# A linear-attention block with a token mixer: the product of Wo with the masked sums from high and low parts, and the steps around it in another order

## The chip, the cores and the metric

The kernel runs on one core of a Trainium2 chip. The metric is the device time of one execution in microseconds (us), the median over several runs. TensorE (PE in the profile; PEld are its weight loads) multiplies matrices, VectorE (DVE), ScalarE (ACT) and GpSimd (POOL) work on elements, and SyncE (SP) starts most of the DMA transfers. Each engine works through its own list of instructions in the order in which the program put them, and semaphores hold an instruction until what it reads is there.

## The reference, cut to what matters

A token array x of 2048 by 448 goes through a linear attention with 16 heads of width 28, and then through an MLP over the tokens. Six vectors of length 448 (shift, scale and gate of each half) come from a condition c.

```
h = layernorm(x) * (1 + ca) + sa
q, k, v = heads of h @ wqkv
phi(t) = where(t > 0, t + 1, exp(t)) + 1e-6
kv  = einsum("bhsd,bhse->bhde", phi(k), v)
z   = einsum("bhsd->bhd", phi(k))
num = einsum("bhqd,bhde->bhqe", phi(q), kv)
den = einsum("bhqd,bhd->bhq", phi(q), z)[..., None] + 1e-6
x = x + ga * ((num / den) @ wo)
h = layernorm(x) * (1 + cb) + sb
u = gelu(einsum("bsd,sf->bdf", layernorm(h), w1) + b1)
x = x + gb * transpose(einsum("bdf,fs->bds", u, w2) + b2)
```

## The kernel before, in words

The 2048 tokens are 16 tiles of 128 rows; an index behind a name is the tile (pkh14 is that of tile 14) or the group. There is no scheduler: each engine executes its instructions in the order in which the code issues them, so the place of a call in the code is its place in the queues of all engines that it uses. SBUF tiles come from two rings (`slot` and `tslot`), PSUM from eight banks (`bank`).

Most products are made from two parts of each operand: `split` (lines 82 to 84) lets ACT write a high part in the type fp32r and DVE write what is left, the low part. High times high, high times low and low times high are then three matmuls with fp32r operands. A matmul with plain fp32 operands needs no split; in the trace each such matmul of 448 columns is two records.

The parts that matter here, in the order of the program:

- The loop over t from 4 to 15 (line 682 on) projects the keys (`kp`), makes phi(k) (`ek`, `rk`, `pk`), its high and low parts (`pkh`, `pkl`), normalizes x (`xn`) and splits it (`xh`, `xl`), and lets PE add phi(k) transposed times x into four banks, `cacc` (`a_outer`, line 554). At the start of a step some early queries are finished (`a_phi_q`: `eq` and `rq` on ACT, `pq` on DVE, lines 465 to 470). At the end of steps 13, 14 and 15 DVE multiplies one group of 112 rows of Wo with the gate (line 779); the fourth group follows behind the loop (line 791).
- Behind the loop come the last four `a_outer`, the sum `pk` of all phi(k) and its parts `zh` and `zl`, and with them the matmuls `zp` (line 799). ACT scales the four banks (`cs`, line 808), DVE adds a correction, and PE multiplies with the V columns of wqkv into the bank `kvb` (line 818). DVE masks it: `kvm` (line 822), the sums within each head.
- Four fp32 matmuls multiply `kvm` with Wo (`wp`, line 968). ACT copies each result to SBUF (`wpg`, line 970), eight DMAs on SP's queue (line 977) rearrange the rows into `wpr`, and each of its four parts is split into `wph` and `wpl` (`wp_split`).
- The loop over i from 0 (line 988 on) takes one query tile per turn. PE transposes the scaled phi(q) (`tq`, line 863), multiplies it with the parts of `wpr` (`op`, lines 893 and 900), and still projects some queries (`qp`). For the tile i + 1 DVE makes `pd`, `den`, the reciprocal and the scaled phi(q) `pn` (lines 836 to 850); GpSimd adds a constant to `den` in between (line 843). The transpose of the tile then reads `pn` as its stationary operand. From turn 5 on PE also adds the first four blocks of the MLP (`up`, lines 950 to 952).
- The weights w1 of the MLP arrive as pieces `pr` of 128 by 512 (`load_to`) and are split into `ph` and `pl` (`split_to(n)` splits all pieces up to the n-th). Pieces 0 to 7 are split ahead of the query loop, in pairs: at line 794 (0, 1), after `zb` (2, 3), after two query projections (4, 5), and after `kvm` (6, 7).
- The scaled phi(q) of tile 0 is made behind `kvm` and behind pieces 6 and 7, just ahead of the four matmuls with Wo.

The MLP's other blocks and its second product fill the rest, from about 190 us to the end; the change does not touch them.

Of the kernel before, what the change touches and what calls it, by code (L numbers as in the profile page):

```python
# [9 lines left out]
F32R = mybir.dt.float32r  # L10
# [8 lines left out]
G = 112  # L19
# [32 lines left out]
def block_kernel(ctx: ExitStack, tc: tile.TileContext, x, xt, wqkv, wo, w1, b1, w2, c, wmod, wfirst, out):  # L52
# [19 lines left out]
    def tslot(name, dt=F32, parts=P, w=D):  # L72
        return tok.tile([parts, w], dt, name=name, tag="tok", padded_shape=[P, 512])


    def moving(new, name, dt=F32R, parts=P):
        return new(name, dt=dt, parts=parts, w=512)[:, 16:16 + D]

    def bank(name):
        return psum.tile([P, 512], F32, name=name, tag="bank")  # L80

    def split(full, hi, lo):
        nc.scalar.activation(hi, full, AF.Copy)  # L83
        nc.vector.tensor_sub(lo, full, hi.bitcast(F32))  # L84
# [219 lines left out]
    def load_to(i):  # L304
        while done["load"] < min(i, len(pieces)):
            k = done["load"]
            t, m, f0, n = pieces[k]
            raws[k] = slot(f"pr{k}", 512)
            nc.sync.dma_start(raws[k].rearrange("p (t f) -> p t f", t=m),
                              w1[t * P:(t + m) * P, f0 * P:(f0 + n) * P].rearrange("(t p) f -> p t f", p=P))  # L310
            done["load"] += 1
# [173 lines left out]
    def a_phi_q(keep=0):  # L485
        a_exp_q(keep)
        for t in sorted(eqs):
            pq[t] = phi_q(t)
# [28 lines left out]
    def a_pk_parts(t):  # L517
        if t not in pks:
            a_pk_high(t)
        a_pk_low(t)  # L520
# [156 lines left out]
    low()  # L677
    sum_end()
    a_split(7)
    wo_sb = []  # L680
    late = [t for t in range(NT) if t not in Q_EARLY.values()]
    for t in range(4, NT):
        if 5 < t < NT - 1:
            project(t + 1, 1, "kp")
        kp = close(t, 1) if t > 4 else kps[4]
        if t == 9:
            row_sum(0)
            row_bias(0)
        if t > 4:
            a_outer(t - KV_LAG)  # L690
        if t % 2 and 4 < t < NT - 2:
            a_transpose(t + 1)
        if t in Q_EARLY:
            a_q(Q_EARLY[t])
        if t == 12:
            mp = mod_sum2(2)
        pair = t % 2 and 7 < t + 3 < NT
        if pair:
            first, second, end = a_stats_dve((t + 3, t + 4))
            first(0)  # L700
        if 5 <= t < 9:
            w_low(0, t - 5)
        if pair:
            second(0)
        if 5 <= t < 9:
            row_part(0, t - 5)
        a_phi_q(t in Q_EARLY)
        if t == 9:
            a_exp(t, kp)
        if t % 2 and 4 < t < NT - 2:  # L710
            a_copy(t + 1)
            a_copy(t + 2)
        if t != 9:
            a_exp(t, kp)
        if 7 < t + 3 < NT:
            a_split_high(t + 3)
        a_pk_parts(t - 1)
        highs = HIGH_AT.get(t, (t - 2,))
        for i in highs[:1]:
            a_norm(i)  # L720
            a_high(i)
        if t % 2 == 0 and 4 < t < NT - 3:
            low = a_rows(t + 2)
        if t == 11:
            low2 = mod_high(2)
        for j, i in MOD_AT.get(t, ()):
            mod_add(j) if i is None else mod_part(j, i)
        if t == 14:
            low4()
        a_pk(t, kp)  # L730
        if t % 2 == 0 and 4 < t < NT - 3:
            low()
        if 7 < t + 3 < NT:
            a_split_low(t + 3)
        for i in highs[1:]:
            a_norm(i)
            a_high(i)
        if pair:
            first(1)
        for i in highs:  # L740
            a_low(i)
        if pair:
            second(1)
            end()
        sum_end()
        if 4 <= t < 8:
            w_high(0, t - 4)
            if t == 7:
                w_row(0)
        if t == 9:  # L750
            row_out(0)
        if t == 12:
            mod_out(2, mp)
            make_mask()
        if t in FETCH:
            load_xt(FETCH[t])
            load_x(FETCH[t])
        if 7 <= t < 11:
            mod_part(2, t - 7)
        if t == 10:  # L760
            mod_add(2)
        if t == 11:
            low2()
        if t == 13:
            low4 = mod_high(4)
        if t in (7, 10):
            load_mod(4 if t == 7 else 3)
        if t == 10:
            load_qkv(2, tslot)
        if t == 8:  # L770
            for g in range(4):
                w = tslot(f"wo{g}", parts=G)
                nc.sync.dma_start(w, wo[g * G:(g + 1) * G, :])
                wo_sb.append(w)
            b12 = cst.tile([P, NF + NT], F32, name="b12")
            nc.sync.dma_start(b12, b1)
            b1c, b2c = b12[:, :NF], b12[:, NF:]
        if t >= 13:
            nc.vector.tensor_mul(wo_sb[t - 13], wo_sb[t - 13], mods[2][:G])
        load_to(PRE_LOAD.get(t, 0))  # L780


    a_pk_parts(NT - 1)
    nc.vector.tensor_add(pksum[1], pksum[1], pksum[0])
    zs = (moving(slot, "zh"), moving(slot, "zl"))
    split(pksum[1], *zs)
    load_to(10)
    a_phi_q()
    a_outer(NT - 4)
    a_outer(NT - 3)  # L790
    nc.vector.tensor_mul(wo_sb[3], wo_sb[3], mods[2][:G])
    for i in (2, 3):
        mod_part(3, i)
    split_to(2)
    a_outer(NT - 2)
    a_outer(NT - 1)
    zp = bank("zp")
    for i, pk in enumerate(zs):
        nc.tensor.matmul(zp[:, :D], ones_r, pk, start=(i == 0), stop=(i == 1))
    zb = tslot("zb")  # L800
    nc.scalar.activation(zb, zp[:, :D], AF.Copy, bias=S * 1e-6)
    load_to(14)
    split_to(4)
    a_q(late.pop(0))
    csum = []
    for ch in range(4):
        csum.append(slot(f"cs{ch}"))
        nc.scalar.activation(csum[ch], cacc[ch][:, :D], AF.Identity, scale=col[1][:, ch:ch + 1])
        nc.vector.scalar_tensor_tensor(csum[ch], zb, col[0][:, ch:ch + 1], csum[ch], op0=ALU.mult, op1=ALU.add)
    a_phi_q()  # L810
    a_q(late.pop(0))
    split_to(6)
    mp = mod_sum2(4)
    kvb = bank("kvb")
    for ch in range(4):
        for g in range(4):
            s = slice(g * G, (g + 1) * G)
            nc.tensor.matmul(kvb[:G, s], raw_w[2, ch][:, s], csum[ch][:, s], start=(ch == 0 and g == 0),  # L818
                             stop=(ch == 3), skip_group_check=True)
    a_phi_q()  # L820
    kvm = slot("kvm", parts=G)
    nc.vector.tensor_mul(kvm, kvb[:G, :D], mask)
    mod_out(4, mp)
    load_to(PRE + MID + 3)
    split_to(8)
    Wpr, Wph, Wpl = [], [], []


    H2h, H2l = [None] * NT, [None] * NT
    pns, phs, ys, opb, sums, nms, nm2s, rss, vss = {}, {}, {}, {}, {}, {}, {}, {}, {}  # L830

    dens, prods, lasts = {}, {}, {}

    def b_prod(t):
# [13 lines left out]
    def b_scale(t):  # L848
        pn = pns.pop(t, None) or tslot(f"pn{t}", w=512)
        nc.vector.scalar_tensor_tensor(pn[:, :D].rearrange("p (h d) -> p h d", d=DH),  # L850
                                       pq[t].rearrange("p (h d) -> p h d", d=DH), 1e-6,
                                       dens.pop(t).unsqueeze(2).to_broadcast([P, H, DH]),
                                       op0=ALU.add, op1=ALU.mult)
        pns[t] = pn
        pq[t] = None

    def b_transpose(t):
        pn = pns.pop(t)
# [101 lines left out]
            del parts[k]  # L960

    a_q(late.pop(0))
    for fn in (b_prod, b_sum, b_eps, b_recip, b_scale):
        fn(0)
    mod_add(3)
    for g in range(4):
        wp = bank(f"wp{g}")
        nc.tensor.matmul(wp[:G, :D], kvm[:, g * G:(g + 1) * G], wo_sb[g], start=True, stop=True)  # L968
        wpg = tslot(f"wpg{g}", parts=G)
        nc.scalar.activation(wpg, wp[:G, :D], AF.Copy)  # L970
        if g == 0:
            Wpr += [tslot(f"wpr{ch}") for ch in range(4)]
        for ch in range(4):
            r0, r1 = max(ch * P, g * G), min(ch * P + P, (g + 1) * G)
            for p0 in (0, 64) if ch == 3 else (0,):
                if r0 < r1:
                    nc.sync.dma_start(Wpr[ch][p0 + r0 - ch * P:p0 + r1 - ch * P], wpg[r0 - g * G:r1 - g * G])
# [10 lines left out]
    for i in range(NT + LAG):  # L988
# [72 lines left out]
        if i == 0:  # L1061
            for ch in range(4):
                wp_split(ch)
        a_phi_q(nq if late else 0)
        load_to(max(14 + (i + 1) // 2, 12 + max(0, i - 6) + max(0, i - 14)))
        if res or norm1:
# [320 lines left out]
```

## Time and profile before

| what | value |
|---|---|
| time, median of 3 runs | 433.37 us (433.33 to 433.41) |
| the profiled execution's own time | 434.09 us |
| its span, first to last instruction | 432.4 us |
| share of the span with PE busy | 99% |
| share with DVE busy | 84% |
| share with ACT busy | 65% |

Times in rows of the trace count from the start of the span. A row of the timeline gives start, length, engine, line, operation, what it writes and reads, shapes and count, and in brackets how long the engine had been idle before and what it had waited for. Records of matmuls overlap: each lasts longer than the distance to the next, and the distance is what counts.

### The profile page before, as it was taken

How to read it: one execution, taken by the hardware profiler on the slowest of the kernel's cores; microseconds unless marked ns; L12 is line 12 of the kernel's file. 1: busy time of each engine (PE TensorE's matmuls, PEld its weight loads, DVE VectorE, ACT ScalarE, POOL GpSimd, SP SyncE). 2: the span in 40 equal slices, each digit the busy share in tenths (PEclk: the TensorE clock that was granted, in tenths of full speed). 3: DMA queues.
4: the chain of work that ended last, by engine and by line, in shares of the span. 5: the costliest groups of instructions: out<-in, count | busy, mean ns of one | idle time of the engine just before them, and what ended most of it. 6: DMA issues, size and time to landing. Idle time of an engine off the chain costs nothing.

```text
span 432.4 us, 7216 instructions
## 1 busy us (share of the span) xinstructions
PE 427.9 (99%) x2331; PEld 398.0 (92%) x2331; DVE 365.1 (84%) x814; ACT 278.9 (65%) x595; POOL 120.1 (28%) x199
## 2 busy tenths in 40 slices
PE   8999999999999999999999999999999999999997
PEld 8888899999899999999999999999999999999996
DVE  4899987889899999998579695739799998898894
ACT  5799869658578899996755263537464664655550
POOL 4345444300026577775200000010113131132010
PEclk9999999999999999999999999999999999999999
DMA  8997997565300036354427461577379977986431
GB/s 282 385 337 162 239 264 162 89 206 193 86 1 0 26 74 148 74 125 97 145 85 244 142 212 50 166 203 210 79 193 214 207 159 159 214 170 144 85 46 41
DMA packets 63797, 66.14 MB, mean 153 GB/s; under 512 B 4816, under 2 KB 55312, under 8 KB 63760
## 3 DMA queue, kind: packets, MB, share of 16 engines
q1 hardware_dynamic: 54688, 50.90, 37.8%
q0 software_dynamic: 8784, 14.32, 20.8%
q10 hardware_dynamic: 288, 0.46, 0.4%
q8 instruction: 18, 0.29, 0.3%
q14 instruction: 19, 0.16, 0.1%
HBM read 46.30 MB, written 7.34 MB: 124 GB/s over the span
## 4 chain that ended last, share of the span: by engine, by line
PE 97%; DVE 1%; ACT 1%; issue 0%
PE y L1183 19%; PE up L951 10%; PE up L950 10%; PE up L952 10%; PE y L1184 9%; PE cacc L554 7%; PE qp L432 7%; PE op L893 7%; PE kp L432 6%; PE op L900 1%; PE warm L188 1%; PE tq L863 1%; PE qp L439 1%; PE kvb L818 1%; PE wp L968 1%; PE rowb L287 1%
## 5 line engine op out<-in xcount | busy, mean ns | idle before, releaser
L950 PE MATMUL up<-h2h,ph 128*128 128x448 f32 x224 | 81.2, 362 | 0.0
L951 PE MATMUL up<-h2l,ph 128*128 128x448 f32 x224 | 81.2, 362 | 0.0
L952 PE MATMUL up<-h2h,pl 128*128 128x448 f32 x224 | 80.8, 361 | 0.0
L1138 POOL DMA_DIRECT2D a<-a x16 | 14.2, 964 | 142.6 <-DMA pr<-in_B_w_dram 76.7
L950 PEld LDWEIGHTS up<-h2h,ph 128*128 128x128 f32 x224 | 42.0, 188 | 3.1
L952 PEld LDWEIGHTS up<-h2h,pl 128*128 128x128 f32 x224 | 41.9, 187 | 3.0
L951 PEld LDWEIGHTS up<-h2l,ph 128*128 128x128 f32 x224 | 42.0, 188 | 2.3
L84 DVE TENSOR_TENSOR pl<-pr,ph 128x512 fp32r<-128x512 f32 x46 | 30.7, 688 | 2.6 <-ACT ph L83 1.7
L1189 ACT ACTIVATE cc<-y 128x448 f32<-128x448 f32 x24 | 13.0, 546 | 26.7 <-PE y L1184 26.7
L1102 DVE TENSOR_TENSOR u<-u,mod 128x448 f32<-128x448 f32 x14 | 8.7, 623 | 23.0 <-ACT u L1101 22.8
L83 ACT ACTIVATE ph<-pr 128x512 fp32r<-128x512 f32 x46 | 27.6, 623 | 0.8 <-PE up L952 0.5
L1101 ACT ACTIVATE u<-up,b 128x448 f32<-128x448 f32 x14 | 8.8, 625 | 25.4 <-PE up L952 24.9
L432 PE MATMUL kp<-wh,hh 128*128 128x448 f32 x64 | 23.8, 377 | 0.0
L554 PE MATMUL cacc<-pkh,xh 128*128 128x448 f32 x64 | 23.6, 369 | 0.0
L432 PE MATMUL qp<-wh,hh 128*128 128x448 f32 x64 | 23.5, 368 | 0.0
L1203 POOL DMA_DIRECT2D out_dram<-yt x14 | 12.7, 909 | 37.3 <-DVE yt L1194 27.9
L843 POOL TENSOR_SCALAR den<-den 128x16 f32<-128x16 f32 x16 | 8.8, 548 | 44.2 <-DVE den L840 44.2
L554 PE MATMUL cacc<-pkl,xh 128*128 128x448 f32 x56 | 20.3, 362 | 0.0
L893 PE MATMUL op<-wph,pth 128*128 128x448 f32 x48 | 18.7, 390 | 0.0
L1144 DVE TENSOR_TENSOR a<-a,s 128x512 f32<-128x512 f32 (+1 forms) x32 | 18.5, 622 | 0.0
L83 ACT ACTIVATE s2h<-s 128x512 fp32r<-128x512 f32 (+1 forms) x16 | 8.3, 569 | 15.5 <-DVE s L1144 15.5
L1183 PE MATMUL y<-ub,a11h 128*128 128x448 f32 x56 | 18.2, 375 | 0.0
(235 smaller groups left out, 1383.7 us busy)
## 6 DMA issues: line engine op xcount, KB each, us to landing
pr<-in_B_w_dram SPq DMA_DIRECT2D x56, 256.0 KB, 3.1
a<-in_B_w_dram SPq DMA_DIRECT2D x32, 256.0 KB, 4.8
a<-in_B_w_dram SPq DMA_DIRECT2D x32, 192.0 KB, 4.7
xt<-in_xt_dram SPq DMA_DIRECT2D x16, 256.0 KB, 5.0
x<-in_A_x_dram SPq DMA_DIRECT2D x16, 224.0 KB, 5.0
wm<-in_B_wmod_dram SPq DMA_DIRECT2D x16, 196.0 KB, 5.2
out_dram<-x SPq DMA_DIRECT2D x14, 224.0 KB, 2.3
out_dram<-yt POOLq DMA_DIRECT2D x14, 224.0 KB, 6.1
```

The lines of the kernel that those rows point to most:

```text
L83: nc.scalar.activation(hi, full, AF.Copy)
L84: nc.vector.tensor_sub(lo, full, hi.bitcast(F32))
L432: nc.tensor.matmul(pps[t, j][:, :D], a[:, ch * P:(ch + 1) * P], w, start=first, stop=False)
L554: nc.tensor.matmul(cacc[ch][:, :D], a[:, s], b, start=(t == 0 and i == 0), stop=(t == NT - 1 and i == len(todo) - 1))
L893: nc.tensor.matmul(opb[t][:, :D], a, b, start=(ch == n == 0), stop=False)
L950: nc.tensor.matmul(ps[:, :D], hi[:, sl], mh, start=first, stop=False)
L951: nc.tensor.matmul(ps[:, :D], hi[:, sl], ml, start=False, stop=False)
L952: nc.tensor.matmul(ps[:, :D], lo[:, sl], mh, start=False, stop=last)
L1138: nc.gpsimd.dma_start(w, a, accum_op=ALU.add)
L1144: nc.vector.tensor_tensor(w, raw2[q, a][i], raw2[q, b][i], op=op)
L1183: nc.tensor.matmul(ps[:, :D], h[:, s], w, start=opens and r == 0, stop=False, skip_group_check=True)
L1184: nc.tensor.matmul(ps[:, :HD], l[:, s], wh, start=False, stop=closes and r == PAIRS - 1, skip_group_check=True)
```

## The change

The four fp32 matmuls of Wo become twelve fp32r matmuls. For this the four groups of Wo are split (`wo_split`: `woh` on ACT, `wol` on DVE), groups 0 and 1 at the end of step 14 of the first loop, right behind the multiplication of group 1, groups 2 and 3 behind `zb`, where pieces 2 and 3 were split. `kvm` is split into `kvh` and `kvl`. Group 3 of Wo is multiplied earlier, between the sum `pk` and `zl`. The five steps of the scaled phi(q) of tile 0 (`b_prod` to `b_scale`) move ahead of and around `kvm`. Pieces 2 to 5 are split behind `kvl`; pieces 6 and 7 in the query loop's turn 0, behind `wpl2` and behind `wpl3`.

```diff
+    def wo_split(g):
+        wos.append((moving(slot, f"woh{g}", parts=G), moving(slot, f"wol{g}", parts=G)))
+        split(wo_sb[g], *wos[g])
...
         if t >= 13:
             nc.vector.tensor_mul(wo_sb[t - 13], wo_sb[t - 13], mods[2][:G])
+        if t == 14:
+            wo_split(0)
+            wo_split(1)
...
     nc.vector.tensor_add(pksum[1], pksum[1], pksum[0])
+    nc.vector.tensor_mul(wo_sb[3], wo_sb[3], mods[2][:G])
     zs = (moving(slot, "zh"), moving(slot, "zl"))
     split(pksum[1], *zs)
...
-    nc.vector.tensor_mul(wo_sb[3], wo_sb[3], mods[2][:G])
...
     load_to(14)
-    split_to(4)
+    wo_split(2)
+    wo_split(3)
...
-    split_to(6)
+    b_prod(0)
+    b_sum(0)
+    b_eps(0)
     mp = mod_sum2(4)
...
     a_phi_q()
+    b_recip(0)
+    mod_out(4, mp)
     kvm = slot("kvm", parts=G)
     nc.vector.tensor_mul(kvm, kvb[:G, :D], mask)
-    mod_out(4, mp)
+    b_scale(0)
+    kvh, kvl = slot("kvh", dt=F32R, parts=G), slot("kvl", dt=F32R, parts=G)
+    split(kvm, kvh, kvl)
     load_to(PRE + MID + 3)
-    split_to(8)
+    split_to(6)
...
     a_q(late.pop(0))
-    for fn in (b_prod, b_sum, b_eps, b_recip, b_scale):
-        fn(0)
     mod_add(3)
+    wps = [bank(f"wp{g}") for g in range(4)]
+    for gs in ((0, 1), (2,), (3,)):
+        for i, (a, b) in enumerate(((kvh, 0), (kvh, 1), (kvl, 0))):
+            for g in gs:
+                nc.tensor.matmul(wps[g][:G, :D], a[:, g * G:(g + 1) * G], wos[g][b], start=(i == 0), stop=(i == 2))
     for g in range(4):
-        wp = bank(f"wp{g}")
-        nc.tensor.matmul(wp[:G, :D], kvm[:, g * G:(g + 1) * G], wo_sb[g], start=True, stop=True)
+        wp = wps[g]
...
             for ch in range(4):
                 wp_split(ch)
+                split_to(max(6, 5 + ch))
```

How the instructions stand then, at three places. First ACT's list at the turn from step 14 to step 15 of the first loop, before (`xh13` and `xh14` are the high parts of x of tiles 13 and 14, `eq4` and `rq4` belong to an early query, `ek15`, `rk15` and `pkh14` to phi(k)):

```order
L500 ACTIVATE xh13_1241<-xn13_1239 128x448
L465 ACTIVATE eq4_1266<-qp4_1212,mv4_416 128x448
L466 ACTIVATE rq4_1267<-qp4_1212,mv4_416 128x448
L446 ACTIVATE ek15_1272<-kp15_1189,mv14_989 128x448
L449 ACTIVATE rk15_1273<-kp15_1189,mv14_989 128x448
L515 ACTIVATE pkh14_1276<-pk14_1245 128x448
L500 ACTIVATE xh14_1283<-xn14_1281 128x448
```

and the same place now:

```order
L500 ACTIVATE xh13_1241<-xn13_1239 128x448
L83 ACTIVATE woh0_1250<-wo0_784 112x448
L83 ACTIVATE woh1_1254<-wo1_786 112x448
L465 ACTIVATE eq4_1274<-qp4_1212,mv4_416 128x448
L466 ACTIVATE rq4_1275<-qp4_1212,mv4_416 128x448
L446 ACTIVATE ek15_1280<-kp15_1189,mv14_989 128x448
L449 ACTIVATE rk15_1281<-kp15_1189,mv14_989 128x448
L515 ACTIVATE pkh14_1284<-pk14_1245 128x448
L500 ACTIVATE xh14_1291<-xn14_1289 128x448
```

The high parts of Wo's groups 0 and 1 stand ahead of everything that step 15 does on ACT. `wo1_786` is what DVE writes at the very end of step 14.

Second, ACT's list between the scale vector `mod4` and the copies `wpg` of the products with Wo, before:

```order
L203 ACTIVATE mod4_1477<-modp4_1450 128x448
L83 ACTIVATE ph6_1485<-pr6_1316 128x512
L83 ACTIVATE ph7_1489<-pr7_1318 128x512
L970 ACTIVATE wpg0_1516<-wp0_1514 112x448
L970 ACTIVATE wpg1_1525<-wp1_1523 112x448
```

and now:

```order
L203 ACTIVATE mod4_1481<-modp4_1455 128x448
L83 ACTIVATE kvh_1487<-kvm_1483 112x448
L83 ACTIVATE ph2_1497<-pr2_1306 128x512
L83 ACTIVATE ph3_1501<-pr3_1308 128x512
L83 ACTIVATE ph4_1505<-pr4_1321 128x512
L83 ACTIVATE ph5_1509<-pr5_1323 128x512
L988 ACTIVATE wpg0_1542<-wp0_1526 112x448
L988 ACTIVATE wpg1_1549<-wp1_1527 112x448
```

Ahead of `wpg0` stood two pieces that need nothing from `kvm`; now there stand `kvh`, which needs `kvm`, and four pieces behind it.

Third, DVE's list in turn 0 of the query loop, before (`wpl` are the low parts of the rearranged product, `pq7` a query, `pd2`, `den2` and `ptl1` steps of the next query tiles):

```order
L84 TENSOR_TENSOR wpl2_1610<-wpr2_1520,wph2_1609 128x448
L84 TENSOR_TENSOR wpl3_1614<-wpr3_1521,wph3_1613 128x448
L470 SCALAR_TENSOR_TENSOR pq7_1617<-eq7_1589,rq7_1590 128x448
L836 SCALAR_TENSOR_TENSOR pd2_1663<-pq2_1151,zb_1382 128x448
L840 TENSOR_REDUCE den2_1665<-pd2_1663 128x16
L878 TENSOR_TENSOR ptl1_1647<-tq1_1619,pth1_1646 128x384
```

and now:

```order
L84 TENSOR_TENSOR wpl2_1630<-wpr2_1546,wph2_1629 128x448
L84 TENSOR_TENSOR pl6_1634<-pr6_1325,ph6_1633 128x512
L84 TENSOR_TENSOR wpl3_1638<-wpr3_1547,wph3_1637 128x448
L84 TENSOR_TENSOR pl7_1642<-pr7_1327,ph7_1641 128x512
L470 SCALAR_TENSOR_TENSOR pq7_1645<-eq7_1609,rq7_1610 128x448
L796 SCALAR_TENSOR_TENSOR pd2_1691<-pq2_1151,zb_1390 128x448
L800 TENSOR_REDUCE den2_1693<-pd2_1691 128x16
L894 TENSOR_TENSOR ptl1_1675<-tq1_1647,pth1_1674 128x384
```

One low part of a piece has come between `wpl2` and `wpl3`, one between `wpl3` and the steps of the next tiles.

More of the change, by code (lines that the diff above doesn't have):

```diff
@@ L679, in block_kernel @@
     a_split(7)
-    wo_sb = []
+    wo_sb, wos = [], []
+    def wo_split(g):
+        wos.append((moving(slot, f"woh{g}", parts=G), moving(slot, f"wol{g}", parts=G)))
+        split(wo_sb[g], *wos[g])
     late = [t for t in range(NT) if t not in Q_EARLY.values()]
@@ L779, in block_kernel @@
             nc.vector.tensor_mul(wo_sb[t - 13], wo_sb[t - 13], mods[2][:G])
+        if t == 14:
+            wo_split(0)
+            wo_split(1)
         load_to(PRE_LOAD.get(t, 0))
[L783 to L790, printed above, removed]
-    nc.vector.tensor_mul(wo_sb[3], wo_sb[3], mods[2][:G])
[L792 to L802, printed above, removed]
-    split_to(4)
[L804 to L811, printed above, removed]
-    split_to(6)
[L813 to L822, printed above, removed]
-    mod_out(4, mp)
-    load_to(PRE + MID + 3)
-    split_to(8)
-    Wpr, Wph, Wpl = [], [], []
-    H2h, H2l = [None] * NT, [None] * NT
-    pns, phs, ys, opb, sums, nms, nm2s, rss, vss = {}, {}, {}, {}, {}, {}, {}, {}, {}
+    pns = {}
     dens, prods, lasts = {}, {}, {}
```

41 lines of the change are left out of this document (added).

## The prediction

> **What bounds the kernel now.** I read the page first: the engines' shares, the granted clock, and the chain of waits that ended last.
>
> ```profile
> span 432.4 us, 7216 instructions
> PE 427.9 (99%) x2331; PEld 398.0 (92%) x2331; DVE 365.1 (84%) x814; ACT 278.9 (65%) x595; POOL 120.1 (28%) x199
> PEclk9999999999999999999999999999999999999999
> PE 97%; DVE 1%; ACT 1%; issue 0%
> ```
>
> PE is busy for 99% of the span at full clock, and the chain is PE for 97%. So whatever PE saves is saved, if the others keep up; and every wait that PE newly gets is paid in full, because nothing behind it has a gap to absorb it. The question is therefore how near the other engines are to making PE wait around the change. The timeline by engine tells. PE first, at the product with Wo (`wp`):
>
> ```profile
> 108.44 0.37 PE L439 MATMUL qp<-wrow,hl 98*128 98x448 f32 x1
> 108.65 3.17 PE L968 MATMUL wp<-wo,kvm 112*112 112x448 f32 x8
> 111.65 0.49 PE L863 MATMUL tq<-ident,pn 128*128 128x128 f32 x3
> ```
>
> The four fp32 matmuls (eight records) hold PE from 108.65 to 111.65, 3.00 us. Then, from another answer, the two matmuls that read what DVE finishes last at the end of the first loop, the third of `a_outer(14)` and the second of `zp`:
>
> ```profile
> 94.26 0.36 PE L554 MATMUL cacc<-pkh,xl 128*128 128x448 f32 x1
> ...
> 98.46 0.36 PE L799 MATMUL zp<-zl,ones_r 128*128 128x448 f32 x1
> ```
>
> Between them lie 21 matmuls: one fp32r matmul of 448 columns takes 4.20 / 21 = 0.20 us.
>
> **What a wait of PE costs.** One of the few waits in the trace, early, on the same pair of operands:
>
> ```profile
> 30.11 0.55 DVE L506 TENSOR_TENSOR xl<-xn,xh 128x384 fp32r<-128x384 f32 x1
> ...
> 30.71 0.19 PEld L554 LDWEIGHTS cacc<-pkh,xl 128*128 128x128 f32 x1 [0.51 <-DVE xl L506]
> ...
> 31.02 0.37 PE L554 MATMUL cacc<-pkh,xh 128*128 128x448 f32 x1
> ```
>
> `xl` ends at 30.66, its weight load starts 0.05 later, and the next matmul at 31.02, where it would stand if the waiting one had begun at 30.82. So a matmul counts as begun 0.16 us after its operand is there.
>
> **The product itself.** Twelve matmuls at 0.20 are 2.40 us in place of 3.00: PE gains 0.60. No row shows an fp32r matmul with 112 rows and 112 weight columns; the nearest is L439 above, 98 rows and 448 columns, 0.21 to the next. The other bound is the old record, 3.00 / 8 = 0.375: twelve would cost 4.50, a loss of 1.50. I take 0.20, by the nearer row.
>
> **The split of groups 0 and 1 holds up ACT.** In ACT's list `woh1` now stands ahead of `eq4`, and it needs the gated group 1, DVE's last step of turn 14. ACT and DVE at that place, before:
>
> ```profile
> 87.28 0.62 ACT L465 ACTIVATE eq<-qp,mv 128x448 f32<-128x448 f32 x1
> ...
> 89.36 0.59 ACT L515 ACTIVATE pkh<-pk 128x448 fp32r<-128x448 f32 x1
> 91.66 0.58 ACT L500 ACTIVATE xh<-xn 128x448 fp32r<-128x448 f32 x1 [1.71 <-DVE xn L496]
> ...
> 96.28 0.58 ACT L83 ACTIVATE zh<-pk 128x448 fp32r<-128x448 f32 x1 [2.62 <-PE cacc L554]
> 96.76 1.13 ACT L83 ACTIVATE ph<-pr 128x512 fp32r<-128x512 f32 x2
> ```
>
> ```profile
> 88.58 0.62 DVE L779 TENSOR_TENSOR wo<-wo,mod 112x448 f32<-112x448 f32 x1
> ...
> 89.98 0.62 DVE L525 SCALAR_TENSOR_TENSOR pkl<-pk,pkh 128x448 fp32r<-128x448 f32 x1 [0.24 <-ACT pkh L515]
> ...
> 91.06 0.51 DVE L496 TENSOR_SCALAR xn<-x,mv 128x448 f32<-128x448 f32 x1
> ...
> 92.57 0.55 DVE L506 TENSOR_TENSOR xl<-xn,xh 128x384 fp32r<-128x384 f32 x1
> ...
> 96.89 0.63 DVE L84 TENSOR_TENSOR zl<-pk,zh 128x448 fp32r<-128x448 f32 x1 [0.70 <-ACT zh L83]
> ```
>
> Group 1 is gated at 88.58 + 0.62 = 89.20. ACT follows DVE by 0.09 (`xn` ends at 91.57, `xh` starts at 91.66), so `woh1` starts at 89.29; the next instruction follows 0.48 later (96.28 to 96.76), so `eq4` starts at 89.77 instead of 87.28: 2.49 us late. Behind it stand `rq4`, `ek15`, `rk15` and `pkh14` without a gap. DVE's `pkl14` started 0.03 after `pkh14`, so it is 2.49 late too, and with it `xn14`, which `xh14` waits for, then `xl14`, and so on to `zl`: DVE's rows there follow one another and name no wait that would absorb it, up to the sum of `pk`; then DVE waits for `zh`, which is as late. The two low parts `wol0` and `wol1` (0.53 us each) lie in the hole that DVE now has; group 3's multiplication fills the 0.70 ahead of `zl`. Both cost nothing.
>
> `xl14` now ends at 93.12 + 2.49 = 95.61 and its matmul counts from 95.77, not 94.26: PE waits 1.51. `zl` ends at 97.52 + 2.49 = 100.01, its matmul counts from 100.17, not 98.46: 1.71 in all. With the 0.60 gained, PE is 1.11 us late behind the product with Wo.
>
> The other two splits of Wo, behind `zb`, replace two pieces on the same engines (448 columns for 512) and ahead of `cs`, so they cost nothing there. SP's list of transfers is unchanged in order, and its last piece ahead of the `wpr` transfers waits for an early query, done long before `wpg0`.
>
> **The tail of the rearranged product holds up DVE.** The mean rows of the page, then ACT, SP, DVE and PE from the timeline:
>
> ```profile
> L84 DVE TENSOR_TENSOR pl<-pr,ph 128x512 fp32r<-128x512 f32 x46 | 30.7, 688 | 2.6 <-ACT ph L83 1.7
> L83 ACT ACTIVATE ph<-pr 128x512 fp32r<-128x512 f32 x46 | 27.6, 623 | 0.8 <-PE up L952 0.5
> ```
>
> ```profile
> 109.60 0.55 ACT L970 ACTIVATE wpg<-wp 112x448 f32<-112x448 f32 x1 [2.45 <-PE wp L968]
> ...
> 117.05 0.58 ACT L83 ACTIVATE wph<-wpr 128x448 fp32r<-128x448 f32 x1 [0.66 <-DMA wpr<-wpg]
> ```
>
> ```profile
> 110.17 5.12 SPq L977 DMA_DIRECT2D wpr<-wpg  x8
> ```
>
> ```profile
> 99.29 2.49 DVE L84 TENSOR_TENSOR pl<-pr,ph 128x512 fp32r<-128x512 f32 x4
> ...
> 106.68 0.63 DVE L822 TENSOR_TENSOR kvm<-kvb,mask 112x448 f32<-112x448 f32 x1 [0.24 <-issue]
> ...
> 117.66 0.63 DVE L84 TENSOR_TENSOR wpl<-wpr,wph 128x448 fp32r<-128x448 f32 x1 [0.61 <-ACT wph L83]
> ...
> 120.21 0.56 DVE L878 TENSOR_TENSOR ptl<-tq,pth 128x384 fp32r<-128x384 f32 x1 [0.20 <-ACT pth L874]
> ...
> 127.01 0.63 DVE L850 SCALAR_TENSOR_TENSOR pn<-pq,den 128x448 f32<-128x448 f32 x1
> ...
> 132.28 0.62 DVE L850 SCALAR_TENSOR_TENSOR pn<-pq,den 128x448 f32<-128x448 f32 x1
> ```
>
> ```profile
> 128.42 0.60 PE L863 MATMUL tq<-ident,pn 128*128 128x128 f32 x4
> 133.29 0.49 PE L863 MATMUL tq<-ident,pn 128*128 128x128 f32 x3
> ```
>
> The eight transfers leave SP one behind the other for 5.12 us from the end of `wpg0`, and `wph3` waits for the last. From `wpl3` at 117.66 to `pn4` at 132.28 DVE has only the 0.20 us of idle time shown. And PE's transposes are close behind: `pn3` ends at 127.64, 0.78 ahead of its transpose, `pn4` at 132.90, 0.39 ahead. With the 0.16 that leaves 0.62 and 0.23 us to spare. DVE is the second bound here.
>
> `kvm` is made when PE has made `kvb`, so it moves by PE's 1.71 to 108.39. `kvh` starts at 108.39 + 0.63 + 0.09 = 109.11, `ph2` 0.48 later, the other three pieces each 1.13 - 0.62 = 0.51 later, and `wpg0` 0.51 behind the last: 111.63 instead of 109.60, 2.03 late (`wp0`, its fifth matmul begun at 108.65 + 1.71 + 0.80 = 111.16, ends near 111.52: just covered). The steps of tile 0 that DVE does ahead of `kvm` may add a tenth. So the transfers, `wph3` and `wpl3` are 2.03 late; `pl6` fits in the 0.61 of idle time ahead of `wpl3`. Behind it `pl7` adds (2.49 - 0.69) / 3 = 0.60, and the 0.20 ahead of `ptl1` is used up: DVE is 2.43 late. The transpose of tile 3 can then be 2.43 - 0.62 = 1.81 late, that of tile 4 is 2.43 - 0.23 = 2.20 late. PE, 1.11 late behind Wo, waits ahead of the transposes for the rest, 1.09 in all. Behind tile 4 the same waits are shorter than what PE has already lost.
>
> The pieces themselves are needed much later, from 142.5 on:
>
> ```profile
> L950 PE MATMUL up<-h2h,ph x224: 360/363/373, 142.5 to 305.1; 128*128 128x448 f32 x112
> ```
>
> **The sum.** +2.20 us. The profiled execution's own time of 434.09, 0.72 above the median, becomes 436.3; the median of 433.37 becomes 435.6. A measurement of this kernel can tell about 0.2%, 0.87 us, from no change.
>
> **The rivals.**
> - Everything fits after all, and the gain stays: faster. For this PE's waits for ACT and DVE must have room that the rows don't show. For it speaks that ACT idles 1.71 us ahead of `xh14` and 2.62 ahead of `zh`; against it, that both idle stretches are waits for DVE, which itself waits for ACT's `pkh14`. The point from which it decides is `xl14`: up to 0.98 us late it costs nothing. 433.37 - 0.60 = 432.8. Chance 0.07.
> - The hold of ACT is paid, but the tail on DVE is covered, for instance because the transfers run closer: 433.37 + 1.11 = 434.5. Chance 0.10.
> - ACT is not held, only the tail is late: `kvm` stays at 106.68, `wpg0` comes at 109.92, 0.32 late; 0.32 + 0.60 - 0.20 - 0.23 = 0.49: 433.9. Chance 0.04.
> - The tail is worse: `ph6` or `pl6` does not fit ahead of `wph3` and `wpl3`, and a further 0.6 to 0.9 comes on top: 436.3. (Were the twelve matmuls as dear as the old records, PE alone would be 1.71 + 1.50 = 3.21 late, 436.6; I count that here.) Chance 0.09.
> - PE's clock drops after the new waits. At the start, before the clock was granted, weight loads were 0.37 apart:
>
> ```profile
> 9.32 0.33 PEld L432 LDWEIGHTS kp<-wh,hl 128*128 128x128 f32 x1
> 9.69 0.33 PEld L432 LDWEIGHTS kp<-wl,hh 128*128 128x128 f32 x1
> ```
>
> If that lasted as long as at the start, where the row at 9.69 is still slow, some ten microseconds hold 27 matmuls, each 0.17 late: 4.6 us on top, 440.2. The wait at 30.71 cost no clock: the next matmul came in the usual time. Chance 0.02. The Trainium skill (TensorE: Matmul & The Clock Gate, HAM oscillation) says that PE falls back to half clock after idle gaps of more than about 3.4 us. By that rule none of the waits here, the longest 1.5 us with a weight load between, would trip it; no run here shows such a gap.
>
> **How the numbers follow.** The forecast has 0.68. Its own range is 435.2 to 436.1: ACT's lateness is sure to a tenth or two, DVE's room to as much. The range for 8 in 10 reaches down to the case of the hold alone and up to the worse tail: 434.3 to 436.5. Faster is the first rival, 0.07. Within 0.2% ends at 434.24 and holds the third rival and part of the second, 0.08. Slower is the rest, 0.85.
>
> **What would show it.** In the profile after: ACT idle ahead of `woh1` on DVE's multiplication near 87.8, and `eq4` near 89.8; PE waiting at `a_outer(14)` for `xh14` and `xl14`, some 1.5 us, and a little for `zl`; twelve `wp` matmuls 0.20 apart; `wpg0` near 111.6; DVE without idle time from `wpl3` to `pn4`; PE waiting ahead of the transposes of tiles 3 and 4. If PE has no wait near 94 us, the first step is wrong; if it has none ahead of the transposes, the second.

## The result, and the profile after

| | before | after |
|---|---|---|
| time, median (range) | 433.41 us (433.33 to 433.42, 5 runs) | 437.14 us (436.59 to 438.11, 5 runs) |
| the profiled execution's own time | 434.09 us | 437.14 us |
| its span | 432.4 us | 435.4 us |

The ratio is 1.0088, with a 95% interval of 1.0073 to 1.0103: 3.7 us slower, where +2.2 was predicted and 436.5 was the top of the range.

The two profiles are first laid over each other. PE's last transpose of a row of weights ahead of the changed code stands at 78.06 in the profile of before and at 77.73 in that of after:

```profile
78.06 0.27 PE L404 MATMUL rw<-ident,rowst 128*98 128x128 f32 x1
```

```profile
77.73 0.27 PE L404 MATMUL rw<-ident,rowst 128*98 128x128 f32 x1
```

So 0.33 is added to every time of after before it is compared; "late" below always means this. (In the twelve profiles this mark lies between 77.19 and 78.72: executions differ at the start already, which goes into the scatter of single runs and falls out of this comparison.) The last matmul, before and after:

```profile
429.07 0.27 PE L1184 MATMUL y<-ut,a22l 128*128 128x224 f32 x1
```

```profile
432.14 0.27 PE L1203 MATMUL y<-ut,a22l 128*128 128x224 f32 x1
```

It is 432.14 + 0.33 - 429.07 = 3.40 us late (3.41 without rounding, as in the table below).

The page of after, engines and chain:

```profile
PE 428.2 (98%) x2335; PEld 395.7 (91%) x2335; DVE 367.9 (84%) x819; ACT 281.6 (65%) x600; POOL 120.4 (28%) x199
...
PE 79%; DVE 7%; DMA 6%; ACT 5%; issue 1%; SPq 0%; POOL 0%; ACTq 0%; DVEq 0%
```

PE is as busy as before, but the chain is PE for 79% only; DVE, ACT and DMA have links in it. Where PE waits, in its summary of waits (line, what it waited for, us in total, times, longest):

```profile
PE op L916 <- DVE pth L901: 0.8, 1, 0.8
PE cacc L554 <- ACT xh L500: 0.7, 1, 0.7
PE tq L879 <- DVE pn L810: 0.6, 2, 0.3
PE cacc L554 <- DVE xl L506: 0.3, 1, 0.3
```

The rows of `cacc` belong to the end of the first loop, the other two to the first query tiles. The hold of ACT, DVE's gate of group 1 that it waits for, and PE at the same place:

```profile
86.96 0.56 ACT L83 ACTIVATE woh<-wo 112x448 fp32r<-112x448 f32 x1
88.97 0.58 ACT L83 ACTIVATE woh<-wo 112x448 fp32r<-112x448 f32 x1 [1.44 <-PE cacc L554]
89.45 0.62 ACT L465 ACTIVATE eq<-qp,mv 128x448 f32<-128x448 f32 x1
```

```profile
88.25 0.62 DVE L784 TENSOR_TENSOR wo<-wo,mod 112x448 f32<-112x448 f32 x1
```

```profile
94.39 0.47 PE L554 MATMUL cacc<-pkh,xh 128*128 128x448 f32 x1 [0.69 <-ACT xh L500]
95.34 0.47 PE L554 MATMUL cacc<-pkh,xl 128*128 128x448 f32 x1 [0.28 <-DVE xl L506]
...
99.98 0.36 PE L432 MATMUL qp<-wh,hh 128*128 128x448 f32 x1
```

(The bracket of `woh1` names a matmul of PE, which ran on there without a gap. But the gate of group 1 ends at 88.25 + 0.62 = 88.87, and `woh1` starts 0.10 later, as it does, to a hundredth, in all five profiles in which the split stands at this place: the gate is the wait.) The query projection behind `zl`, before:

```profile
98.66 0.36 PE L432 MATMUL qp<-wh,hh 128*128 128x448 f32 x1
```

It is 99.98 + 0.33 - 98.66 = 1.65 late. Then the product with Wo, first group and first transpose:

```profile
109.98 0.57 PE L984 MATMUL wp<-woh,kvh 112*112 112x448 f32 x2
...
112.44 0.49 PE L879 MATMUL tq<-ident,pn 128*128 128x128 f32 x3
```

2.46 us for the twelve, in place of 3.00. PE is 112.44 + 0.33 - 111.65 = 1.12 late. So far the profile is the prediction's. Then the tail, ACT, SP and DVE:

```profile
111.59 1.82 ACT L988 ACTIVATE wpg<-wp 112x448 f32<-112x448 f32 x4
...
115.37 0.57 ACT L83 ACTIVATE wph<-wpr 128x448 fp32r<-128x448 f32 x1
116.20 0.58 ACT L83 ACTIVATE wph<-wpr 128x448 fp32r<-128x448 f32 x1 [0.26 <-DMA wpr<-wpg]
117.73 0.58 ACT L83 ACTIVATE wph<-wpr 128x448 fp32r<-128x448 f32 x1 [0.95 <-DMA wpr<-wpg]
...
120.12 0.58 ACT L83 ACTIVATE wph<-wpr 128x448 fp32r<-128x448 f32 x1 [1.29 <-DMA wpr<-wpg]
```

```profile
112.14 5.09 SPq L995 DMA_DIRECT2D wpr<-wpg  x8
```

```profile
108.02 0.25 DVE L806 RECIPROCAL den<-den 128x16 f32<-128x16 f32 x1 [0.17 <-POOL den L803]
108.30 0.62 DVE L861 TENSOR_TENSOR kvm<-kvb,mask 112x448 f32<-112x448 f32 x1
...
120.73 0.63 DVE L84 TENSOR_TENSOR wpl<-wpr,wph 128x448 fp32r<-128x448 f32 x1 [1.17 <-ACT wph L83]
121.28 0.69 DVE L84 TENSOR_TENSOR pl<-pr,ph 128x512 fp32r<-128x512 f32 x1
121.88 0.62 DVE L470 SCALAR_TENSOR_TENSOR pq<-eq,rq 128x448 f32<-128x448 f32 x1
...
135.67 0.63 DVE L810 SCALAR_TENSOR_TENSOR pn<-pq,den 128x448 f32<-128x448 f32 x1
```

`wpg0` is 111.59 + 0.33 - 109.60 = 2.32 late, the transfers 2.30, but `wph3` 120.12 + 0.33 - 117.05 = 3.40: between the transfers' start and their landing another 1.1 us has come in. The view of the transfers by tile says where, first before, then after (from issue to landing, least, median, most):

```profile
DMA to landing us min/median/max: 2.0/2.3/2.6
```

```profile
DMA to landing us min/median/max: 2.0/2.3/3.4
```

The transfer with 3.4 is the eighth. What came in its way is a packet of instructions: PE gets its instructions by DMA, 16 KB at a time, on a queue of its own (q8 in the views; that it is PE's is what the warm-up kernels below show). The DMA view of after for 117.9 to 119.9 us, busy share and rate in slices of 0.05 us, and what ran there:

```profile
DMA  9397497682111000002000200020020000000000
GB/s 507 108 358 179 108 323 251 179 215 72 36 36 36 0 0 0 0 0 36 0 0 0 36 0 0 0 36 0 0 36 0 0 0 0 0 0 0 0 0 0
...
q8 instruction: 1, 0.02, 2.9%
```

At the left edge, at 117.91, stands one packet of instructions of 16 KB. Its 2.9% of 16 engines over 2 us are 0.93 us, so it ends at 118.84. The transfer's data is through by 118.6, except for four single packets, some 0.2 us apart, from 118.8 to 119.4. The transfer's 64 rows on 16 DMA engines are four rows each: these are one engine's share. The trace does not name the engine of a packet. That the four rows stood behind the instruction packet on its engine is read from the times: the first of them starts when that packet ends, here and in each of the four other profiles below in which the two meet.

In the profile of before the same packet comes alone, at 117.45, behind the last transfer, whose data was through by 116.6. Its view for 116 to 118 us:

```profile
DMA  8798986941200000000000000000090000000000
...
q8 instruction: 1, 0.02, 2.9%
```

The prediction does not mention this packet.

### The profile page after: what moved, and what is told of

It reads as the page before. It is cut to its first block, busy times and chain, and to the rows that moved or that the text cites. A ratio compares the mean times of both kernels' runs of the same rounds, so it can differ in the third digit from the quotient of the medians.

```text
span 435.4 us, 7232 instructions
## 1 busy us (share of the span) xinstructions
PE 428.2 (98%) x2335; PEld 395.7 (91%) x2335; DVE 367.9 (84%) x819; ACT 281.6 (65%) x600; POOL 120.4 (28%) x199
## 4 chain that ended last, share of the span: by engine, by line
PE 79%; DVE 7%; DMA 6%; ACT 5%; issue 1%; SPq 0%; POOL 0%; ACTq 0%; DVEq 0%
PE y L1202 19%; PE up L967 10%; PE up L966 10%; PE up L968 10%; PE y L1203 9%; PE op L909 5%; PE cacc L554 4%; PE kp L432 4%; DMA xt<-in_xt_dram 2%; PE qp L432 2%; DMA wr<-in_qkv_dram 2%; PE op L916 1%; PE tq L879 1%; DMA pr<-in_B_w_dram 1%; DMA wpr<-wpg 1%
```

## The experiments

Two theories stood at the start. A: three losses, one behind the other: the hold of ACT, the tail on DVE, and the instruction packet in the way of the last transfer. B, in several forms: one of the three is not real (the last transfer is slow for itself; the hold is only cover; DVE's own work sets the end whatever comes ahead).

All numbers together. "Late" is PE against the profile of before, as above. The last column is the time from issue to landing: of the slowest of the eight transfers where one took 3 us or more, and of the eighth (the median of the last two) where none did. The slowest is the eighth, except in the two kernels with two queues ("two queues" and "fitted, second"), where it is one in the middle.

| kernel | median us | ratio to before (95%) | late at tile 0 | at tile 4 | at the end | landing |
|---|---|---|---|---|---|---|
| changed, again | 437.59 | 1.0091 (1.0077 to 1.0105) | 1.09 | 3.85 | 3.87 | 3.9 |
| no hold | 436.29 | 1.0062 (1.0048 to 1.0076) | -0.52 | 2.41 | 2.43 | 3.8 |
| pieces 6, 7 later | 437.77 | 1.0095 (1.0081 to 1.0109) | 1.11 | 3.34 | 4.04 | 4.0 |
| two queues | 435.79 | 1.0054 (1.0040 to 1.0068) | 1.11 | 2.22 | 2.26 | 3.7 |
| changed, short warm-up | 436.33 | 1.0061 (1.0047 to 1.0074) | 1.11 | 2.24 | 2.27 | 2.3 |
| before, short warm-up | 433.88 | 1.0005 (0.9996 to 1.0014) | 0.00 | 0.00 | 0.00 | 2.2 |
| before, long warm-up | 434.19 | 1.0011 (1.0001 to 1.0021) | -0.01 | 1.03 | 1.05 | 3.9 |
| no hold, short warm-up | 435.28 | 1.0032 (1.0019 to 1.0044) | -0.49 | 0.85 | 0.89 | 2.2 |
| fitted | 433.25 | 0.9990 (0.9982 to 0.9999) | -0.26 | -0.21 | -0.23 | 2.3 |
| fitted, second | 433.76 | 0.9998 (0.9989 to 1.0007) | -0.52 | -0.24 | -0.21 | 3.8 |

The kernel before had 433.45 us beside the first four, 433.51 beside the short and long warm-ups of the two kernels and the fitted one, and 433.79 beside the last two kernels run (no hold with short warm-up; fitted, second).

**The changed kernel again**, without an edit.

> The changed kernel once more, nothing edited, for a second profile and more times. In its first profile the eighth transfer into the rearranged product took 3.41 us from issue to landing where the median of the eight was 2.3, and a 16 KB packet of instructions ran at 117.9, just while that transfer was under way. Theory A: the packet in the way of the last transfer is what made it 1.1 us late, and with it everything on DVE up to the scaled phi(q) of tile 4; whether they meet changes from execution to execution, and that is the scatter of the times (436.6 to 438.1). Then this profile shows either the meeting again and a landing of about 3.4 us with a span near 435.4, or no meeting, a landing of 2.3 to 2.6 and a span some 1 us shorter. Theory B: the last transfer is slow for itself (its place as the last of eight); it lands after 3.4 us whatever the packet does, and the scatter comes from elsewhere.

The meeting came again, at 117.33, and the landing was 3.9. So far B could stand as well: the last transfer was late both times. The guess that they meet in some executions and not in others finds no support: they met in both profiles, and again in those of "no hold" and "pieces 6 and 7 later". In these four the packet starts as the eighth transfer's first rows do, within some hundredths of a microsecond; which of the two sets the other's moment the trace does not tell. So the scatter of the times (436.6 to 438.1) stays unexplained. In all eight profiles with six warm-up matmuls the packet came between 116.0 and 117.9.

**No hold.**

```diff
-        if t == 14:
-            wo_split(0)
-            wo_split(1)
...
     split(pksum[1], *zs)
+    wo_split(0)
+    wo_split(1)
```

> The high and low parts of Wo's groups 0 and 1 are made behind the parts of the sum of phi(k) instead of at the end of step 14; all else is as in the changed kernel. ACT then waits for nothing new in the loop. Theory A (two losses, one behind the other): PE no longer waits for the high and low part of x of tile 14 and for zl (0 instead of 1.65 us in all), the masked sums come about 1.4 us earlier, and the tail moves with them: copies of the product with Wo from 110.4, the time 434.4, or 435.5 where a packet of instructions makes the last transfer 1.1 us late. Theory B (DVE's own work from the masked sums to tile 4 sets the end, whatever comes ahead): the hold is only cover, DVE loses its idle time instead, and the time stays above 436.5.

Between the two. PE has no wait in the loop and is 0.52 ahead at tile 0, so the hold is real; at the end 1.0 to 1.4 of its 1.65 are gained. The median is 0.8 above the 435.5 that A gave with the packet and 0.2 below B's floor; the meeting came again, and the landing of 3.8 instead of 3.4 is 0.4 of the 0.8. ACT's wait for that transfer:

```profile
119.74 0.58 ACT L83 ACTIVATE wph<-wpr 128x448 fp32r<-128x448 f32 x1 [1.71 <-DMA wpr<-wpg]
```

**Pieces 6 and 7 later.**

```diff
                 wp_split(ch)
-                split_to(max(6, 5 + ch))
...
-        split_to(8 + max(0, i - 5))
+        split_to(min(8, max(6, 3 + i)) + max(0, i - 5))
```

> Pieces 6 and 7 are split at the end of turns 4 and 5 of the query loop instead of between and behind the parts of the rearranged product in turn 0; all else is as in the changed kernel. Theory A (my sum): the low part of piece 7 costs its 0.60 us ahead of the scaled phi(q) of tiles 3 and 4, and behind tile 4 there is room (1.68 us ahead of the transpose of tile 6 before the change): the time falls by 0.6, to 436.5. Theory B: DVE is full in all turns up to tile 15 (0.18 to 0.40 us of room per tile), and what is taken out of turn 0 is paid in turns 5 to 8: the time stays at 437.1 within 0.2.

B, though 437.77 lies above its range and 0.2 above the 437.59 of the changed kernel in the same series. The transfer was as late as in the changed kernel's second profile (4.0 and 3.9), so the two can be compared: PE's lateness at tile 4 is 3.34 instead of 3.85, but between tiles 5 and 8 it gets another 0.6, and a wait that was not there before:

```profile
153.37 0.63 PE L879 MATMUL tq<-ident,pn 128*128 128x128 f32 x4 [0.26 <-DVE pn L810]
```

What the two low parts gave back ahead of tile 4, 0.5 us, they cost again behind it, 0.7.

**Two queues.**

```diff
-                    nc.sync.dma_start(Wpr[ch][p0 + r0 - ch * P:p0 + r1 - ch * P], wpg[r0 - g * G:r1 - g * G])
+                    (nc.gpsimd if g == 2 else nc.sync).dma_start(Wpr[ch][p0 + r0 - ch * P:p0 + r1 - ch * P], wpg[r0 - g * G:r1 - g * G])
```

> The two transfers into the rearranged product that read group 2 start from GpSimd's queue, the other six from SP's as before, so that SP is through with its list two transfers (1.3 us) earlier; all else is as in the changed kernel. Theory A: the tail is set by the last transfer. The last part of the rearranged product then lands 1.3 us earlier or more (2.4 where the instruction packet no longer meets it), PE's waits for the scaled phi(q) of tiles 2 to 4 and for the high parts of tile 1 go or shrink to some tenths, and the time falls by 1.1 to 2.2, to 434.9 to 436.0; what stays is the hold, 1.1. Theory B: DVE's own work in that stretch, not the transfers, is what is late; then DVE's idle time ahead of the low parts goes, but the time stays at 437.1 within 0.4.

The time is in A's range: it falls by 1.35 to 1.8 (against 437.14 and 437.59), and `wph3` starts at 118.36, laid over the profile of after 1.3 earlier. But the edit did two things at once. The views of 117 to 119 us and of the transfers:

```profile
DMA  0100090000000000000000000000000000000000
...
q8 instruction: 1, 0.02, 2.9%
```

```profile
wpr<-wpg POOLq DMA_DIRECT2D x1, 140.0 KB, 3.7
wpr<-wpg SPq DMA_DIRECT2D x1, 84.0 KB, 3.7
```

The packet now comes behind the last transfer, at 117.29, and meets nothing. And PE is 2.26 late at the end, just as with one queue and the packet moved away (2.27, in the next kernels). So what fell is the packet's share; that the shorter list of SP gained anything beyond it is not shown. The transfers of the two queues ran at the same time, and five of the eight took 2.7 to 3.7 us to land, with no instruction packet among them, so that `wph2` was no earlier than with one queue.

**Warm-up matmuls**, three kernels. Each changes only the number of matmuls at the very start.

```diff
-WARM = 6
+WARM = 0
```

> The changed kernel without the first six warm-up matmuls (twelve records at the very start), which write a bank that nobody reads; the result is the same. The packets of instructions of PE came at 117.1 to 117.9 in every profile so far, whatever PE waited for, and 12 records at 0.20 us put this one 2.4 us later, to 119.5 or later, when the last transfer's data has moved (117.9 to 118.5). Theory A (the packet makes the last transfer late): it lands after 2.2 to 2.6 us instead of 3.4 to 4.0, the scaled phi(q) of tiles 2 to 4 come 1.1 to 1.6 us earlier, and the time falls by as much against the changed kernel, less or more what the shorter warm-up costs, which the kernel before with the same edit shows: 435.9 to 436.5. Theory B (the last transfer is slow for itself): landing 3.4 or more, time 437.1 to 437.6.

> The control: the kernel before without the first six warm-up matmuls. Its packet comes behind the last transfer either way (117.45, then some 119.8). Both theories: the landing stays at 2.3 us and the time is 433.4 plus what the shorter warm-up costs or saves at the start, which I put between -0.5 and +1.

And the other way in the kernel before, `WARM = 10`:

> The kernel before with ten instead of six first warm-up matmuls: eight records more, so that PE's packet of instructions comes 1.6 us earlier, at about 115.9 instead of 117.45, while the last transfer's packets ran at 116.0 to 116.6. Theory A: now the kernel before has the late transfer too: landing 3.0 or more, and behind the 0.20 us of idle time and the 0.23 of room at tile 4 some 0.5 to 1.2 us of it reach the end: 433.9 to 434.6, beside what the longer warm-up costs. Theory B: landing 2.3, and no wait of PE for the scaled phi(q).

A in all three, and the packet moved much further than expected (to 124.6 and 121.8, not to about 119.5). With the short warm-up the changed kernel's packet comes at 124.6, and the eighth transfer lands after 2.3 us. ACT's wait for it and the transfers by tile:

```profile
119.04 0.58 ACT L83 ACTIVATE wph<-wpr 128x448 fp32r<-128x448 f32 x1 [0.15 <-DMA wpr<-wpg]
```

```profile
DMA to landing us min/median/max: 2.0/2.3/2.6
```

PE is 2.27 late at the end instead of 3.41 and 3.87: the meeting costs 1.1 to 1.6. With the long warm-up the kernel *before*, which has no hold and no changed tail, gets the same late transfer. Its DMA view from 115.8 to 118.0, ACT's wait, and PE's:

```profile
DMA  9848421000000000000000200200020020000000
...
q8 instruction: 1, 0.02, 3.4%
```

```profile
118.32 0.58 ACT L83 ACTIVATE wph<-wpr 128x448 fp32r<-128x448 f32 x1 [2.34 <-DMA wpr<-wpg]
```

```profile
PE tq L863 <- DVE pn L850: 0.3, 1, 0.3
```

Again four single packets at the end, a landing of 3.9, and 1.05 us at the end of PE. The median is 0.7 above the kernel before beside it, within what cannot be told from no change; the reading rests on the profile. The control, the kernel before with the short warm-up, has neither the late transfer nor a wait of PE. The packets are PE's instructions: nothing but PE's list was edited, and they moved.

**No hold and short warm-up**: both edits together.

> The changed kernel with both taken away: the parts of Wo's groups 0 and 1 behind the parts of the sum of phi(k), and without the first six warm-up matmuls, which put the packet of instructions behind the last transfer (124.61 in the changed kernel, 121.77 in the kernel before). What is left is the tail's own lateness: the steps of tile 0 ahead of the masked sums, four pieces ahead of the first copy, the low part of piece 7. Theory A (three losses that add up: hold, tail, packet): the last transfer lands after 2.3 to 2.6 us, PE is 0.5 us ahead of the kernel before at the first transpose, and waits 1.4 to 1.6 us for tiles 1 to 4; 0.9 to 1.1 us late at the end, 434.4 to 434.7. Theory B (the hold's lateness and the tail's are the same time counted twice, so that taking the hold away gains only what PE gains): as late as without the packet alone, 2.27, 435.8 to 436.3.

A by the profile: PE is 0.49 ahead at tile 0 and 0.89 late at the end. The losses are separate in the main: of the hold's 1.65 us, 2.27 - 0.89 = 1.38 come back, and the rest turns into longer waits of the tail (1.38 in place of 1.16). The median does not fit as well: it lies 0.6 above A's upper end, 1.5 over its own runs of before. The profiled execution started late (the mark near 78 us stands at 78.72, 0.66 later than in the profile of before); whether the others did is not known.

**Fitted.** The twelve matmuls are kept, and what the profiles showed to cost is put elsewhere.

```diff
-PIECE_DMA = range(8, 18)
+PIECE_DMA = range(6, 18)
...
-        if t == 14:
-            wo_split(0)
-            wo_split(1)
...
     split(pksum[1], *zs)
+    wo_split(0)
+    wo_split(1)
...
-    split_to(6)
+    split_to(4)
...
-    for gs in ((0, 1), (2,), (3,)):
+    for gs in ((0,), (1,), (2,), (3,)):
...
-                split_to(max(6, 5 + ch))
+                split_to((4, 5, 6, 6)[ch])
...
-        split_to(8 + max(0, i - 5))
+        split_to(6 + (i > 2) + (i > 3) if i < 6 else 3 + i)
```

> A version that takes away what cost time by the traces, with the twelve matmuls kept: the parts of Wo's groups 0 and 1 behind the parts of the sum of phi(k), only pieces 2 and 3 ahead of the copies of the product with Wo, pieces 4 and 5 between the parts of the rearranged product, where ACT and DVE wait for transfers, pieces 6 and 7 in turns 3 and 4 with their low parts by accumulating DMA instead of DVE, and the twelve matmuls group by group. Theory A: no wait in the loop, copies from 109.3 as against 109.60 before the change; without the meeting of the last transfer and the packet the 0.60 that PE gains is nearly all kept: 432.9 to 433.2. PE passes the place of the packet about a microsecond earlier than before the change, though, so the two may meet: then 1.1 to 1.6 later, 434.0 to 434.8. Theory B (DVE is full in that stretch, whatever the order): DVE has 2.7 us of low parts of Wo and of the masked sums more, 1.2 less of pieces, and 435 or more comes out.

A's mechanism: PE has no wait from the loop to the end of the query tiles, and the packet just misses the last transfer. The time is 433.25 us, 0.05 above A's range and 0.1% less than before: less than the 0.2% that can be told from no change. The order by groups kept half the gain back, since its third matmul waits for `kvl`: the first transpose is 0.26 ahead, not 0.52. The load of its weights:

```profile
108.55 0.17 PEld L983 LDWEIGHTS wp<-woh,kvl 112*112 112x112 f32 x1 [0.39 <-DVE kvl L84]
```

**Fitted, second**: the order of groups as in the changed kernel, and two queues.

> The fitted version with two edits: the twelve matmuls in the changed kernel's order (groups 0 and 1 interleaved), since the order by groups waited for the low part of the masked sums and kept 0.26 of the 0.55 us; and the two transfers that read group 2 on GpSimd's queue, so that the last one lands earlier and DVE keeps pace with PE at tile 4, where the fitted version had 0.11 us of room. Theory A: PE is 0.5 us ahead of the kernel before at the first transpose and stays so: 432.9 to 433.1. Theory B (DVE's work up to tile 8 sets the end): the room at tile 4 or 8 is used up and 0.2 us remain, 433.2 to 433.3.

B's mechanism: PE is 0.52 ahead at tile 0, 0.44 at tile 3, 0.24 at tile 4. DVE takes back what PE gained. The time, 433.76, is above both ranges, but so was the kernel before beside it (433.79), and the two are the same. The two queues did not help here either: transfers took up to 3.8 us to land, and `wph2` started 0.48 late, against 0.11 in the first fitted version. Neither version beats the kernel before, or the other, by a difference that can be told.

## Why the prediction was wrong

The direction, the mechanisms and two of three sizes were right; one term of the tail was too small.

- **The product**: twelve at 0.20, 2.40 in place of 3.00. Measured 2.46, a gain of 0.54.
- **The hold**: `eq4` at 89.77 was predicted; 89.45 + 0.33 = 89.78. PE 1.71 late by `zl`: 1.65. Net behind Wo 1.11: 1.12. Without the hold it is -0.52. Right.
- **`kvm` and `wpg0`**: 108.39 and 111.63 were predicted, 108.63 and 111.92 measured. "The steps of tile 0 that DVE does ahead of `kvm` may add a tenth": they add 0.24, because the reciprocal stands ahead of `kvm` and waits 0.17 for GpSimd. Small here, larger in the rival "only the tail is late", which took `kvm` to stay at 106.68 and gave 0.49. Without hold and packet `kvm` starts 0.60 late, and the end is 0.89 late.
- **The step that failed**: "the transfers, `wph3` and `wpl3` are 2.03 late". The transfers are 2.30 late, `wph3` is 3.40. The prediction moved the eight transfers as a block and took their landing time along unchanged, as if nothing else ran on the DMA engines there. But a block that is moved in time meets other traffic. Moved by 2.3 us, the last transfer meets PE's instruction packet, and 1.1 (3.40 - 2.30) to 1.6 us are added; the edits of the warm-up show it from both sides. The profile of before had the packet in it, at 117.45, less than a microsecond behind the last transfer's data.
- **The sum without the packet**: the changed kernel is then 2.27 late, where the sum said 2.20. That it is so near is in part luck, two errors against each other. DVE comes to `pn4` 2.57 late, not 2.43 (in the profile with the short warm-up, where 0.27 is added to lay it over, `pn4` starts at 134.58: 134.58 + 0.27 - 132.28). And PE's transpose of tile 4 had 0.39 - 0.06 = 0.33 us to spare before, not 0.23: where it waits, as it does in the profiles of after, it starts 0.06 behind the end of `pn4`, and not the 0.16 that the prediction took from a matmul early in the kernel.
- **Piece 7 and DVE behind it**: 0.60 at 121.28, and no idle time from there to `pn4`. Right in size. "Behind tile 4 the same waits are shorter than what PE has already lost" held too: PE is 3.38 late at tile 4 and 3.41 at the end. It does not mean that there is room for more work behind tile 4: put into turns 4 and 5, the low parts cost PE 0.7 us.
- **Where PE waits**: tiles 3 and 4 were named. It waits for DVE before that already: 1.11 late at the transpose of tile 1, it is 2.52 late at that of tile 2, 3.08 and 3.38 at 3 and 4, because DVE comes behind `wpl3` 3.4 late and not 2.0. (Tile 2 was passed over in the sum: also without the packet its transpose is 1.38 late.) Two of its rows of after, tiles 2 and 3 (before: 123.47 and 128.42):

```profile
125.67 0.55 PE L879 MATMUL tq<-ident,pn 128*128 128x128 f32 x3 [0.24 <-DVE pn L810]
131.17 0.63 PE L879 MATMUL tq<-ident,pn 128*128 128x128 f32 x4 [0.32 <-DVE pn L810]
```

- **The rivals**: "the tail is worse" (0.09) was the one nearest in size, 436.3 to 436.6, but by another mechanism, pieces that do not fit; `ph6` and `pl6` did fit. No rival had another queue's traffic in it. The clock stayed at full speed; behind the start no wait of PE was longer than 1.4 us (no hold), so the rule on idle gaps was not tried.

The 3.7 us as they came out one behind the other, in the profiles: hold 1.65, product -0.54, waits of the tail 1.16 (2.27 - 1.11), packet 1.14 in the first profile and 1.60 in the second, 3.41 and 3.87. The medians differ by 3.73.

Open: what sets the moment of a packet. Twelve records of PE fewer moved it from 117.9 to 124.6 in the changed kernel and from 117.45 to 121.8 in the kernel before, eight more moved it forward by 1.6: not one rule by the count. Nor is it shown how the tail's 1.16 divide between the pieces ahead of `wpg0` and piece 7: the fitted version took them away together. It kept the steps of tile 0 ahead of `kvm`, which starts 0.60 late there too. Nor was it tried what the low parts of Wo would cost on GpSimd instead of DVE.

## What to carry to other kernels

When a chain of small transfers moves in time, look at what else runs on the DMA engines at its new place, the instruction packets included: a landing time holds for its place only. Where PE and a second engine are both without room over a long stretch, a gain of PE is worth only as much as the second engine can follow (here 0.52 us at tile 0 were 0.21 at the end), and work moved within the stretch gained nothing here. When an edit brings a time that a theory gave, look in the trace whether it came by the theory's way: the two queues shortened a list and moved the transfers out of the packet's way at once. An engine's list is held up by the first instruction that waits, so what needs another engine's last step belongs behind everything that does not.

## What the runs showed of the hardware

- A 16 KB packet of instructions of PE takes a DMA engine for 0.9 to 1.5 us in this stretch, and a transfer spread over the engines lands 1.1 to 1.7 us later if its rows there are behind the packet (3.4 to 4.0 in place of 2.3). There are 18 such packets in each execution, and in the profiles read here only the one that meets the last of the eight transfers was seen to cost time. All 18, from the page of before:

```profile
q8 instruction: 18, 0.29, 0.3%
```

The Trainium skill (Runtime: NRT & Kernel Launch, Instruction fetch mechanics) says that instructions come in blocks of 16 KiB by a DMA queue of the sequencer's own and that the cost of crossing a block is mostly hidden. The 0.29 MB in 18 packets agree with the blocks. Hidden it is for PE, which shows no wait for it; for a data transfer on the same DMA engine it is not. The Trainium skill (DMA: Bandwidth & Descriptors, Queues, rings and completion order) says that a DMA engine takes turns between its queues packet by packet; the four rows that came only after the packet agree.

- Transfers started from two queues at the same time each take longer to land. With two of the eight on GpSimd's queue five took 2.7 to 3.7 us (up to 3.8 in the second fitted version), with all eight on SP's queue and no packet in the way none took more than 2.6.
